# A gated convolution MLP: blocks 0 and 1 scaled in opposite banks, the sums of the first layer split in a new order

## The chip, the cores and the metric

The kernel runs on one core of one Trainium2 chip. The metric is the device time of one execution in microseconds (us). The five engines of the core work side by side, each through its own list of instructions in the order in which it was written: TensorE (PE in the rows; PEld is its loading of weights), VectorE (DVE), ScalarE (ACT), GpSimd (POOL) and SyncE (SP), which here only issues DMAs. They wait for one another through semaphores.

## The reference

Three steps, all in fp32, for 8192 tokens of 192 values. A softmax over 7 taps, for each of 8 heads, weights a causal convolution. Two feed-forward layers follow:

```python
out = np.einsum('bshk,bskhg->bshg', softmax(weight_gen), x_unf)      # 7 taps, 8 heads
xn  = x / np.sqrt(np.mean(x * x, -1) + 1e-06) * rms_g
y   = (silu(xn @ w_gate) * (xn @ w_val)) @ w_out                     # 192 -> 1536 -> 192
h   = y @ w_in                                                       # 192 -> 2048
out = (h * sigmoid(1.702 * h)) @ w_out2                              # 2048 -> 192
```

## The kernel before

The tokens are cut into 16 blocks of 512. TensorE multiplies fp32 numbers as two parts: a high part, rounded to the format `fp32r`, and a low part, the rest. So each operand exists as a pair: `xh`, `xl` and `yh`, `yl` for the first 128 of the 192 values of a token, `xsh`, `xsl` and `ysh`, `ysl` for the other 64, and `h`, `l` for hidden values.

A **unit** `(1, b, m)` is one of 12 pieces of the first layer for block b (function `U1`): TensorE makes `pg` and `pv` in two PSUM banks, ScalarE makes silu of `pg` (line 485), VectorE multiplies by `pv` (`p`, line 489), ScalarE copies the high part (`h`, line 490), VectorE takes the low part (`l`, line 493). A unit `(2, b, i)` is one of 8 pairs of pieces of the second layer (`U2`): two banks `ph`, two silus each (lines 506, 507), one low part each (line 513). The banks of units come from one pool of four, so a unit writes into the banks of the unit two before it, and must wait until that one's have been read. Every product is followed one or two units later by its share of the sums `a` and `b` (`D1`, `D2`).

When the last share of a block's first layer is in, `Y(b)` takes the sums out: ScalarE copies the two halves of bank `b` crosswise into `yt` (lines 537, 538), then bank `a` as `yh` (539), later `yt` as `ysh` (542); VectorE adds bank `b` to `yt` (540) and takes the low parts `yl` (541) and `ysl` (543). `Y(b)` is called at the end of a unit. For blocks from 2 on, two units of the next block's first layer stand between it and the first unit `(2, b, 0)`, which reads its results; the `p` of the first of these two units stands on VectorE behind `Y(b)`, and its banks are those that `(2, b, 0)` writes.

The order of all instructions is that of the code. The list `units` fixes the units; `some` puts steps of other work between their parts on VectorE and ScalarE: decoding the weights (`piece_steps`, lines 95 to 122, while blocks 0 and 1 run) and the convolution of later blocks (`xr`, `acc`, lines 229 and 262). The entries of `splits` run at the end of the unit whose number is their key.

Blocks 0 and 1 open the kernel. Their convolution sums lie in PSUM, tokens 0 and 1 of a row in bank `ac`, tokens 2 and 3 in bank `bc`. `sc(j)` scales them by `ri`: VectorE writes 192 values (line 284), ScalarE another copy of the last 64 (line 287). Then TensorE transposes them into `ax` and `bx`, which use the same two banks (line 351).

Of the kernel before, what the change touches and what calls it, by code (L numbers as in the profile page):

```python
# [9 lines left out]
F32 = mybir.dt.float32  # L10
# [4 lines left out]
ALU = mybir.AluOpType  # L15
# [3 lines left out]
P = 128  # L19
# [5 lines left out]
D = 192  # L25
# [17 lines left out]
def gated_conv_mlp(ctx: ExitStack, tc: tile.TileContext, xp, wg, w1, wo1, w2, wo2, g, out):  # L43
    nc = tc.nc
# [173 lines left out]
    def conv_ops(b):  # L218

        T = BLOCKS[b]  # L220
        Q = T * HEADS
        x = xch[b]
        wn = wn_of[b]
        xr = att.tile([P, T, 2 * P], F32, tag="xr", name=f"xr{b}")
        prod = xr.rearrange("p t c -> p (t c)")[:, 0:Q * GRP]
        ops = []

        def mul(eng, k, dst, j0=0, j1=T):
            eng.tensor_tensor(  # L229
                out=dst.rearrange("p (q g) -> p q g", g=GRP),  # L230
                in0=x[:, (k + j0) * D:(k + j1) * D].rearrange("p (q g) -> p q g", g=GRP),
                in1=wn[:, j0 * HEADS:j1 * HEADS, k:k + 1].to_broadcast([P, (j1 - j0) * HEADS, GRP]), op=ALU.mult)
        cost = 1.04 * Q * GRP + 70
        if b < 2:
            S = T // 2
            sums_of = [pacc.tile([P, NM], F32, tag=f"{n}{b}", name=f"{n}c_{b}") for n in "ab"]
            acc_of = [sums_of[j // S][:, (j % S) * D:(j % S + 1) * D] for j in range(T)]
        else:
            acc = att.tile([P, T, D], F32, tag="acc", name=f"acc{b}")
            acc_of = [acc[:, j] for j in range(T)]  # L240
        if b == 1:
            def tap(k):
                for i, ps in enumerate(sums_of):
                    tag = (("yh", "yl"), ("ysh", "ysl"), ("yh0", "yl0"))[k % 3][i]
                    pr = ytp.tile([P, NM], F32R, tag=tag, name=f"pr{k}_{i}").bitcast(F32)[:, :S * D]
                    mul(nc.gpsimd, k, pr, i * S, (i + 1) * S)
                    nc.tensor.matmul(ps[:, :S * D], ident, pr, start=k == 0, stop=k == TAPS - 1)
            ops += [(cost, lambda k=k: tap(k)) for k in range(TAPS)]
        elif b == 0:
            n = S * D  # L250

            def tap(k):
                for i, ps in enumerate(sums_of):
                    mul(nc.vector, k, prod[:, i * n:(i + 1) * n] if k else ps[:, :n], i * S, (i + 1) * S)
                for i, ps in enumerate(sums_of if k else ()):
                    nc.vector.tensor_tensor(out=ps[:, :n], in0=ps[:, :n], in1=prod[:, i * n:(i + 1) * n], op=ALU.add)
            ops += [(cost, lambda k=k: tap(k)) for k in range(TAPS)]
        else:
            total = acc.rearrange("p t d -> p (t d)")

            def add():
                nc.vector.tensor_tensor(out=total, in0=total, in1=prod, op=ALU.add)  # L262
            for k in range(TAPS):
                ops.append((cost, lambda k=k: mul(nc.vector, k, prod if k else total)))
                if k:
                    ops.append((cost, add))
        ss = sml.tile([P, T], F32, tag="ss", name=f"ss{b}")
        ri = sml.tile([P, T], F32, tag="ri", name=f"ri{b}")

        def sq():  # L270
            room = xr if b != 1 else ytp.tile([P, NM], F32R, tag="yh", name="sq1").bitcast(F32).unsqueeze(1)
            for j in range(T):
                nc.scalar.activation(out=room[:, j if b != 1 else 0, 0:D], in_=acc_of[j], func=AF.Square,
                                     accum_out=ss[:, j:j + 1])
        ops.append((1500, sq))

        def root():
            nc.gpsimd.tensor_scalar(out=ss, in0=ss, scalar1=1.0 / D, scalar2=1e-6,
                                    op0=ALU.mult, op1=ALU.add)
            nc.gpsimd.tensor_tensor(out=ri, in0=ss, in1=half[:, :T], op=ALU.pow)  # L280
        ops.append((500, root))

        def sc(j):
            nc.vector.tensor_scalar_mul(out=xr[:, j, 0:D], in0=acc_of[j], scalar1=ri[:, j:j + 1])
            if b >= TURN:
                return
            nc.scalar.mul(out=xr[:, j, D:2 * P], in_=acc_of[j][:, P:D], mul=ri[:, j:j + 1])
        for j in range(T):
            ops.append((230, lambda j=j: sc(j)))
        xrow[b] = xr  # L290
        return ops
# [79 lines left out]
    yT = {}  # L371
# [144 lines left out]
    def D1(b, m):  # L516
        if m == 0:
            acc1[b] = sums(b, "1_")
        return (acc1[b], O1[m], m, M1, BLOCKS[b] * P, hl1.pop((b, m))), (lambda: Y(b)) if m == M1 - 1 else None
# [6 lines left out]
    def Y(b):  # L526
        N = BLOCKS[b] * P
        pa, pb = acc1.pop(b)
        g = "0" if b in (0, NB - 1) else ""
        W = N if g else NM  # L530
        h = ytp.tile([P, W], F32R, tag="yh" + g, name=f"yh{b}")
        l = ytp.tile([P, W], F32R, tag="yl" + g, name=f"yl{b}")
        sh = ytp.tile([P, W], F32R, tag="ysh" + g, name=f"ysh{b}")
        sl = ytp.tile([P, W], F32R, tag="ysl" + g, name=f"ysl{b}")
        t = zp.tile([P, NM], F32, tag="zb", name=f"yt{b}")

        nc.scalar.copy(t[0:DR, :N], pb[DR:P, :N])
        nc.scalar.copy(t[DR:P, :N], pb[0:DR, :N])
        nc.scalar.copy(h[:, :N], pa[:, :N])
        nc.vector.tensor_tensor(out=t[:, :N], in0=t[:, :N], in1=pb[:, :N], op=ALU.add)  # L540
        nc.vector.tensor_tensor(out=l[:, :N], in0=pa[:, :N], in1=h[:, :N].bitcast(F32), op=ALU.subtract)
        nc.scalar.copy(sh[:, :N], t[:, :N])
        nc.vector.tensor_tensor(out=sl[:, :N], in0=t[:, :N], in1=sh[:, :N].bitcast(F32), op=ALU.subtract)
        yT[b] = (h, l, sh, sl)

    def Z(b, own=None):
        N = BLOCKS[b] * P
# [44 lines left out]
        xt_at[b] = pos[1, b - 1, M1 - 8 if b >= TURN else M1 - 2]  # L592
    xt_by_pos = {v: k for k, v in xt_at.items()}
    splits = {}
    group_of = {b0: gi for gi, (b0, b1) in enumerate(GROUPS)}


# [14 lines left out]
    line = deque()  # L612
# [48 lines left out]
    def some(amounts):  # L661
        for k, a in enumerate(amounts):
            credit[k] += a
        while True:
            ready = [k for k in (0, 1) if streams[k] and credit[k] > 0]
            if not ready:
                return
            for k in ready:
                q = streams[k]
                spent = 0.0  # L670
                while q and credit[k] > 0 and spent < 1500:
                    _, c, f = q.popleft()
                    f()
                    credit[k] -= c
                    spent += c
# [3 lines left out]
    with ExitStack() as order:  # L679
# [49 lines left out]
        soft = {}  # L729
        for i, u in enumerate(units):  # L730
            kind, b, m = u
            if (kind, b, m) == (1, 2, 0):
                early.close()
                late = ctx.enter_context(tc.tile_pool(name="late", bufs=6))
                parts.append((late, late))
                squares.append(ctx.enter_context(tc.tile_pool(name="squares", bufs=1)))
# [40 lines left out]
            while pend and pend[0][0] <= i:  # L777
                _, D_, key = pend.popleft()
                d, f = D_(*key)
# [4 lines left out]
            if i == 0:  # L784
                split = transpose_x(1)
                split(dves=False)
                second()
                split(acts=False)
                third()
                some(todo)  # L790
                some(todo)
            elif i < pos[1, 1, 2]:
                second()
                some(todo)
                third()
                some(todo)
            else:
                some(todo)
                second()
                some(todo)  # L800
                third()
# [4 lines left out]
            else:  # L806

                last = len(units) - 1
# [53 lines left out]
```

## Time and profile before

| | |
|---|---|
| three runs | 1240.44, 1241.30, 1241.46 us; median 1241.3 us |
| the profiled execution | 1240.54 us, of which 1238.6 us are the span from the first to the last instruction |
| busy in the span | PE 1215.7 us (98%), DVE 773.1 us (62%), ACT 650.2 us (52%), POOL 32.3 us (3%) |
| mean granted clock of TensorE | 0.998 of 2.4 GHz |

Busy time is summed over the whole span. It says little of single stages: DVE is busy for 25.6 of the first 31 us and for all 10 us from 30 to 40 us.

### The profile page before, as it was taken

What the parts mean: (1) busy time and instruction counts of PE and PEld (TensorE: products, weight loads), DVE (VectorE), ACT (ScalarE), POOL (GpSimd) and SP (SyncE); (2) the same over time, 40 slices, a digit from 0 to 9 for tenths busy, and PEclk for the clock granted to TensorE, in tenths of its full rate; (3) what the DMA queues carried; (4) which work ended last, traced back from release to release, by engine and by line L of the source; (5) the groups of instructions that cost most, each with busy time, mean ns of one, the idle gap of its engine ahead of it and who ended that gap; (6) DMA issues with size and microseconds to landing.
All of it is one profiled execution on the core that took longest, in us unless ns stands there. A gap on an engine that the chain in (4) does not pass through costs nothing.

```text
span 1238.6 us, 26868 instructions
## 1 busy us (share of the span) xinstructions
PE 1215.7 (98%) x10324; PEld 1100.3 (89%) x10324; DVE 773.1 (62%) x1296; ACT 650.2 (52%) x1279; POOL 32.3 (3%) x53
## 2 busy tenths in 40 slices
PE   5999999999999999999999999999999999999998
PEld 3776999988888999999999989999899998888897
DVE  8989847576657475665747557475664746545432
ACT  4666664555646445454564545446454554544553
POOL 4000000000000000000000000000000000000000
PEclk9999999999999999999999999999999999999999
DMA  5865411001101000110001001001100011000000
GB/s 187 274 182 185 133 57 46 2 1 58 33 16 48 7 25 33 42 34 11 21 33 31 33 16 59 7 26 33 31 33 11 22 33 31 1 15 18 1 14 13
DMA packets 33855, 57.51 MB, mean 46 GB/s; under 512 B 7744, under 2 KB 19392, under 8 KB 33728
## 3 DMA queue, kind: packets, MB, share of 16 engines
q1 hardware_dynamic: 33728, 55.80, 14.5%
q8 instruction: 81, 1.33, 0.4%
q14 instruction: 46, 0.38, 0.1%
HBM read 43.71 MB, written 6.29 MB: 40 GB/s over the span
## 4 chain that ended last, share of the span: by engine, by line
PE 90%; DVE 7%; ACT 2%; issue 1%; DMA 0%; POOL 0%; DVEq 0%; POOLq 0%; ACTq 0%
PE a L380 24%; PE ph L380 21%; PE b L380 16%; PE pv L380 14%; PE pg L380 14%; DVE p L489 1%; DVE l L493 1%; DVE xr L229 1%; DVE dec_a L107 1%; ACT h L490 0%; DVE w L117 0%; DVE dec_s L99 0%; DVE dec_s L111 0%; DVE o L117 0%; DVE acc L262 0%
## 5 line engine op out<-in xcount | busy, mean ns | idle before, releaser
L380 PE MATMUL a<-h,o 64*128 64x512 f32 x1788 | 517.0, 391 | 0.0
L380 PEld LDWEIGHTS a<-h,o 64*128 64x128 f32 x1788 | 326.7, 184 | 14.2
L513 DVE TENSOR_TENSOR l<-p,h 128x512 fp32r<-128x512 f32 x256 | 176.1, 691 | 235.2 <-ACT p L507 233.6
L380 PE MATMUL b<-l,o 64*128 64x512 f32 x896 | 311.2, 393 | 0.1
L380 PE MATMUL a<-l,o 64*128 64x512 f32 x894 | 310.0, 392 | 1.0 <-DVE l L513 0.8
L380 PE MATMUL b<-h,o 64*128 64x512 f32 x896 | 310.4, 392 | 0.0
L506 ACT ACTIVATE h<-ph 128x512 fp32r<-128x512 f32 x256 | 153.9, 601 | 208.5 <-PE ph L380 199.9
L380 PE MATMUL pv<-xh,w 64*128 64x512 f32 x768 | 241.9, 394 | 1.6 <-DVE p L489 1.1
L380 PE MATMUL pg<-xh,w 64*128 64x512 f32 x768 | 242.0, 393 | 1.2 <-ACT w L122 1.2
L380 PE MATMUL ph<-yh,w 64*128 64x512 f32 x1024 | 234.4, 392 | 1.6 <-DVE p L489 1.4
L490 ACT CAST h<-p 128x512 fp32r<-128x512 f32 x192 | 119.4, 622 | 186.3 <-DVE p L489 186.3
L485 ACT ACTIVATE p<-pg 128x512 f32<-128x512 f32 x192 | 114.6, 597 | 164.3 <-PE pg L380 163.7
L489 DVE TENSOR_TENSOR p<-p,pv 128x512 f32<-128x512 f32 x192 | 131.6, 685 | 104.1 <-PE a L380 72.3
L493 DVE TENSOR_TENSOR l<-p,h 128x512 fp32r<-128x512 f32 x192 | 132.6, 691 | 82.9 <-ACT h L490 82.6
L380 PEld LDWEIGHTS a<-l,o 64*128 64x128 f32 x894 | 165.1, 185 | 14.3 <-DVE l L513 2.5
L380 PEld LDWEIGHTS b<-l,o 64*128 64x128 f32 x896 | 165.5, 185 | 8.7 <-DVE l L493 0.5
L380 PEld LDWEIGHTS b<-h,o 64*128 64x128 f32 x896 | 163.9, 185 | 7.7 <-POOLq L395 0.5
L380 PEld LDWEIGHTS ph<-yh,w 64*128 64x128 f32 x1024 | 145.3, 185 | 15.1 <-DVE p L489 2.1
L507 ACT ACTIVATE p<-ph 128x512 f32<-128x512 f32 x256 | 153.9, 601 | 0.0
L380 PEld LDWEIGHTS pv<-xh,w 64*128 64x128 f32 x768 | 140.8, 185 | 14.3 <-DVE p L489 3.8
L380 PE MATMUL ph<-yl,w 64*128 64x512 f32 x512 | 151.2, 391 | 0.0
L380 PE MATMUL pv<-xl,w 64*128 64x512 f32 x384 | 150.5, 392 | 0.0
(117 smaller groups left out, 2098.2 us busy)
## 6 DMA issues: line engine op xcount, KB each, us to landing
x<-in_xp SPq DMA_DIRECT2D x15, 960.0 KB, 4.8
st<-in_w SPq DMA_DIRECT2D x20, 384.0 KB, 4.0
zt<-in_w SPq DMA_DIRECT2D x20, 384.0 KB, 3.4
st<-in_wo SPq DMA_DIRECT2D x14, 384.0 KB, 3.9
zt<-in_wo SPq DMA_DIRECT2D x14, 384.0 KB, 3.4
out_z<-za SPq DMA_DIRECT2D x16, 256.0 KB, 2.2
xl<-raw SPq DMA_DIRECT2D x176, 16.0 KB, 1.8
xsl<-raw SPq DMA_DIRECT2D x176, 16.0 KB, 1.8
```

The lines of the kernel that those rows point to most:

```text
L107: nc.vector.scalar_tensor_tensor(out=ai, in0=ai, scalar=3, in1=t["s"], op0=ALU.logical_shift_left, op1=ALU.bitwise_or)
L229: eng.tensor_tensor(out=dst.rearrange("p (q g) -> p q g", g=GRP), in0=x[:, (k + j0) * D:(k + j1) * D].rearrange("p (q g) -> p q g", g=GRP) ...
L380: ins = nc.tensor.matmul(ps[:, :N], w[rows], x[rows, :N], start=start, stop=stop)
L485: nc.scalar.activation(out=p[:, :N], in_=pg[:, :N], func=AF.Silu)
L489: nc.vector.tensor_tensor(out=p[:, :N], in0=p[:, :N], in1=pv[:, :N], op=ALU.mult)
L490: nc.scalar.copy(h[:, :N], p[:, :N])
L493: nc.vector.tensor_tensor(out=l[:, :N], in0=p[:, :N], in1=h[:, :N].bitcast(F32), op=ALU.subtract)
L506: nc.scalar.activation(out=h[:, :N], in_=ps[j][:, :N], func=AF.Silu, scale=SIG)
L507: nc.scalar.activation(out=p[:, :N], in_=ps[j][:, :N], func=AF.Silu, scale=SIG)
L513: nc.vector.tensor_tensor(out=l[:, :N], in0=p[:, :N], in1=h[:, :N].bitcast(F32), op=ALU.subtract)
```

## The change

Three edits. First, in `sc(j)` of blocks 0 and 1, ScalarE takes token `(j + 2) % 4` while VectorE takes token j, so that the two read different banks. Second, `Y(b)` is written in two parts, `first` (`yh`, `yl`) and `last` (`ysh`, `ysl`). For blocks 0 and 1 both parts are put into `splits` and run at the end of the next unit, only the two crosswise copies and the addition staying where they were. For the other blocks both parts stay in place, `first` ahead of the addition and `last` behind it. Third, at the end of unit 0 the last step of the third weight piece (the copy of its high part, line 122) is run at once, and no longer a unit later.

```diff
@@ sc(j) @@
-            nc.scalar.mul(out=xr[:, j, D:2 * P], in_=acc_of[j][:, P:D], mul=ri[:, j:j + 1])
+            i = (j + T // 2) % T if b < 2 else j
+            nc.scalar.mul(out=xr[:, i, D:2 * P], in_=acc_of[i][:, P:D], mul=ri[:, i:i + 1])
@@ Y(b) @@
         nc.scalar.copy(t[0:DR, :N], pb[DR:P, :N])
         nc.scalar.copy(t[DR:P, :N], pb[0:DR, :N])
-        nc.scalar.copy(h[:, :N], pa[:, :N])
+        yT[b] = (h, l, sh, sl)
+
+        def first():
+            nc.scalar.copy(h[:, :N], pa[:, :N])
+            nc.vector.tensor_tensor(out=l[:, :N], in0=pa[:, :N], in1=h[:, :N].bitcast(F32), op=ALU.subtract)
+
+        def last():
+            nc.scalar.copy(sh[:, :N], t[:, :N])
+            nc.vector.tensor_tensor(out=sl[:, :N], in0=t[:, :N], in1=sh[:, :N].bitcast(F32), op=ALU.subtract)
+        if b > 1:
+            first()
         nc.vector.tensor_tensor(out=t[:, :N], in0=t[:, :N], in1=pb[:, :N], op=ALU.add)
-        nc.vector.tensor_tensor(out=l[:, :N], in0=pa[:, :N], in1=h[:, :N].bitcast(F32), op=ALU.subtract)
-        nc.scalar.copy(sh[:, :N], t[:, :N])
-        nc.vector.tensor_tensor(out=sl[:, :N], in0=t[:, :N], in1=sh[:, :N].bitcast(F32), op=ALU.subtract)
-        yT[b] = (h, l, sh, sl)
+        if b > 1:
+            last()
+        else:
+            splits[at_unit[0] + 1] = lambda: (first(), last())
...
@@ the loop over units @@
+            at_unit[0] = i
...
                 third()
                 some(todo)
                 some(todo)
+                for f in line[0].pop(0):
+                    f()
```

On ScalarE at the start, the list changes in two places: `ac` and `bc` are the banks of the sums of blocks 0 and 1, `w_2` is the third piece's high part, `p_0_1` and `h_0_1` belong to unit (1, 0, 1). Before:

```order
L122 CAST w_0_120<-dec_a 128x384
L287 ACTIVATE xr_156<-ac_157,ri_160 128x64 x2
L287 ACTIVATE xr_156<-bc_158,ri_160 128x64 x2
...
L95 ACTIVATE dec_a<-st 128x384
L485 ACTIVATE p_0_1_413<-pg_1_391 128x512
L490 CAST h_0_1_414<-p_0_1_413 128x512
L122 CAST w_2_259<-dec_a 128x384
```

With the change:

```order
L122 CAST w_0_120<-dec_a 128x384
L288 ACTIVATE xr_156<-bc_158,ri_160 128x64 x2
L288 ACTIVATE xr_156<-ac_157,ri_160 128x64 x2
...
L95 ACTIVATE dec_a<-st 128x384
L122 CAST w_2_259<-dec_a 128x384
L486 ACTIVATE p_0_1_414<-pg_1_392 128x512
L491 CAST h_0_1_415<-p_0_1_414 128x512
```

The two banks have changed places, and the copy of `w_2` stands ahead of the silu and the copy of a unit. VectorE's list is unchanged there.

On VectorE at the end of unit (1, 1, 9), where block 0's sums are taken out. Before:

```order
L493 TENSOR_TENSOR l_1_9_1552<-p_1_9_1550,h_1_9_1551 128x512
L540 TENSOR_TENSOR yt_1576<-yt_1576,b_0_435 128x512
L541 TENSOR_TENSOR yl_1573<-a_0_434,yh_1572 128x512
L543 TENSOR_TENSOR ysl_1575<-yt_1576,ysh_1574 128x512
L229 TENSOR_TENSOR xr_885<-x_663,wraw_311 128x768
L489 TENSOR_TENSOR p_1_10_1620<-p_1_10_1620,pv_10_1585 128x512
L493 TENSOR_TENSOR l_1_10_1622<-p_1_10_1620,h_1_10_1621 128x512
```

With the change:

```order
L494 TENSOR_TENSOR l_1_9_1552<-p_1_9_1550,h_1_9_1551 128x512
L551 TENSOR_TENSOR yt_1576<-yt_1576,b_0_435 128x512
L229 TENSOR_TENSOR xr_885<-x_663,wraw_311 128x768
L490 TENSOR_TENSOR p_1_10_1616<-p_1_10_1616,pv_10_1581 128x512
L494 TENSOR_TENSOR l_1_10_1618<-p_1_10_1616,h_1_10_1617 128x512
L544 TENSOR_TENSOR yl_1573<-a_0_434,yh_1572 128x512
L548 TENSOR_TENSOR ysl_1575<-yt_1576,ysh_1574 128x512
```

`yl` and `ysl` have moved behind the whole next unit, and on ScalarE `yh` and `ysh` likewise behind that unit's `h`. Block 1's move in the same way, behind the two `l` of unit (2, 0, 2).

On VectorE at the end of unit (1, 5, 1), where block 4's sums are taken out. Before:

```order
L493 TENSOR_TENSOR l_5_1_5634<-p_5_1_5632,h_5_1_5633 128x512
L540 TENSOR_TENSOR yt_5644<-yt_5644,b_4_4578 128x512
L541 TENSOR_TENSOR yl_5641<-a_4_4577,yh_5640 128x512
L543 TENSOR_TENSOR ysl_5643<-yt_5644,ysh_5642 128x512
L229 TENSOR_TENSOR xr_5176<-x_5135,wraw_2688 128x768
L489 TENSOR_TENSOR p_5_2_5688<-p_5_2_5688,pv_2_5655 128x512
```

With the change:

```order
L494 TENSOR_TENSOR l_5_1_5634<-p_5_1_5632,h_5_1_5633 128x512
L544 TENSOR_TENSOR yl_5641<-a_4_4577,yh_5640 128x512
L551 TENSOR_TENSOR yt_5644<-yt_5644,b_4_4578 128x512
L548 TENSOR_TENSOR ysl_5643<-yt_5644,ysh_5642 128x512
L229 TENSOR_TENSOR xr_5176<-x_5135,wraw_2688 128x768
L490 TENSOR_TENSOR p_5_2_5688<-p_5_2_5688,pv_2_5655 128x512
```

The low part `yl` and the addition to `yt` have changed places. The same holds for all blocks from 2 to 15; ScalarE's list there is unchanged (`yt`, `yt`, `yh`, `ysh`, and then the silu of the next unit). TensorE's, GpSimd's and SyncE's lists are the same throughout.

## Rows read from the trace of the kernel before

**Rows 1.** The page: span, TensorE's busy time, and the second layer's costliest group.

```profile
span 1238.6 us, 26868 instructions
...
PE 1215.7 (98%) x10324; PEld 1100.3 (89%) x10324; DVE 773.1 (62%) x1296; ACT 650.2 (52%) x1279; POOL 32.3 (3%) x53
...
L380 PE MATMUL ph<-yh,w 64*128 64x512 f32 x1024 | 234.4, 392 | 1.6 <-DVE p L489 1.4
```

**Rows 2.** TensorE's waits from 130 us to the end: total, count, longest.

```profile
PE a L380 <- DVE l L513: 0.5, 1, 0.5
```

**Rows 3.** Windows: length, busy time of PE, PEld, DVE, ACT, POOL, granted clock, DMA.

```profile
24.50:28.50 4.00, 3.98 (x17) 2.59 (x17) 3.35 (x7) 2.36 (x5) 0.00 (x0) 0.57 0.49 133
30.00:40.00 10.00, 8.67 (x72) 7.12 (x72) 10.00 (x25) 6.39 (x15) 0.00 (x0) 1.00 0.68 201
```

**Rows 4.** Timeline of VectorE, scalings of blocks 0 and 1: start, length, [wait before].

```profile
22.88 0.42 DVE L284 TENSOR_SCALAR xr<-ac,ri 128x192 f32<-128x192 f32 x1 [0.38 <-ACT xr L287]
...
24.01 0.42 DVE L284 TENSOR_SCALAR xr<-bc,ri 128x192 f32<-128x192 f32 x1 [0.38 <-ACT xr L287]
...
28.20 0.42 DVE L284 TENSOR_SCALAR xr<-ac,ri 128x192 f32<-128x192 f32 x1 [0.44 <-ACT xr L287]
...
29.32 0.42 DVE L284 TENSOR_SCALAR xr<-bc,ri 128x192 f32<-128x192 f32 x1 [0.38 <-ACT xr L287]
```

**Rows 5.** Timeline of ScalarE and TensorE around the third piece.

```profile
37.44 0.51 ACT L122 CAST w<-dec_a 128x384 fp32r<-128x384 f32 x1
...
38.00 0.50 PE L380 MATMUL pg<-xh,w 64*128 64x512 f32 x1 [1.22 <-ACT w L122]
```

**Rows 6.** Timeline of VectorE and TensorE, block 0's sums.

```profile
108.28 0.69 DVE L540 TENSOR_TENSOR yt<-yt,b 128x512 f32<-128x512 f32 x1 [0.52 <-ACT yt L538]
...
110.27 0.95 DVE L229 TENSOR_TENSOR xr<-x,wraw 128x768 f32<-128x768 f32 x1
111.13 0.68 DVE L489 TENSOR_TENSOR p<-p,pv 128x512 f32<-128x512 f32 x1
...
111.87 0.50 PE L380 MATMUL ph<-yh,w 64*128 64x512 f32 x2 [1.21 <-DVE p L489]
```

**Rows 7.** Timeline of VectorE and TensorE after block 1's sums.

```profile
129.24 1.29 DVE L513 TENSOR_TENSOR l<-p,h 128x512 fp32r<-128x512 f32 x2
...
129.98 0.50 PE L380 MATMUL a<-l,o 64*128 64x512 f32 x1 [0.51 <-DVE l L513]
...
130.59 0.50 PE L380 MATMUL a<-l,o 64*128 64x512 f32 x1
```

**Rows 8.** Timelines of ScalarE, VectorE and TensorE, block 4's sums.

```profile
385.98 0.59 ACT L539 CAST yh<-a 128x512 fp32r<-128x512 f32 x1
386.71 0.62 ACT L542 CAST ysh<-yt 128x512 fp32r<-128x512 f32 x1
...
385.98 0.69 DVE L540 TENSOR_TENSOR yt<-yt,b 128x512 f32<-128x512 f32 x1 [0.51 <-ACT yt L538]
...
387.36 0.69 DVE L543 TENSOR_TENSOR ysl<-yt,ysh 128x512 fp32r<-128x512 f32 x1
387.97 0.95 DVE L229 TENSOR_TENSOR xr<-x,wraw 128x768 f32<-128x768 f32 x1
388.84 0.68 DVE L489 TENSOR_TENSOR p<-p,pv 128x512 f32<-128x512 f32 x1
...
389.70 0.63 PE L380 MATMUL ph<-yh,w 64*128 64x512 f32 x4
```

**Rows 9.** The same two engines, block 13: its `p`, and the product that follows.

```profile
1058.71 0.68 DVE L489 TENSOR_TENSOR p<-p,pv 128x512 f32<-128x512 f32 x1
...
1059.57 0.41 PE L380 MATMUL ph<-yh,w 64*128 64x512 f32 x2
```

**Rows 10.** The same two rows of block 2.

```profile
238.56 0.68 DVE L489 TENSOR_TENSOR p<-p,pv 128x512 f32<-128x512 f32 x1
...
240.28 0.43 PE L380 MATMUL ph<-yh,w 64*128 64x512 f32 x2
```

More of the change, by code (lines that the diff above doesn't have):

```diff
@@ L594, in gated_conv_mlp @@
     splits = {}
+    at_unit = [0]
     group_of = {b0: gi for gi, (b0, b1) in enumerate(GROUPS)}
```

## The prediction

> **What bounds the kernel now.** I read the page first. TensorE is busy for 1215.7 of the 1238.6 us of the span [rows 1], so a change can win at most the 22.9 us that are left, and can lose whatever it adds to TensorE's idle time. Next came TensorE's own waits, to see where those 22.9 us lie: from 130 us to the end there is one, of 0.5 us [rows 2]. So the kernel has two stages. Up to about 131 us TensorE, VectorE and ScalarE wait for one another; afterwards TensorE runs without a gap for 1107 us. Everything that the change could win lies in the first stage. In the second it can only be harmless or harmful, and which of the two depends on how early the other engines deliver. The timelines of the edited places tell that, and they are the rest of the argument.
>
> **The scaling in opposite banks.** VectorE and ScalarE both read the sums, and today they read the same bank by turns: VectorE waits for ScalarE twice in block 0 (0.38 and 0.38 us) and twice in block 1 (0.44 and 0.38 us) [rows 4]. ScalarE's list now begins with the other bank, so these four waits have no cause left: 1.58 us of VectorE's time. This counts, because VectorE is busy without a break right behind them (10.00 of the 10 us from 30 to 40 us [rows 3]); what it starts earlier there it finishes earlier. I take 1.4 us and not 1.58, since ScalarE's next step, a decoding step for which VectorE waits, still stands behind ScalarE's own four scalings. Bounds: 0.8 us, if only block 1's pair of waits (0.82 us) carries through, and 1.6 us.
>
> These waits come from synchronization of the two engines by bank. The Trainium skill (PSUM — Partial Sum Buffer, section on PSUM bank collisions) says that two engines must not be in one bank and the same partitions at once, reads against reads included, while different banks are free. By that rule alone all four waits go, and the sum would be lower by 0.18 us; no row of the kernel before shows the two engines started together in opposite banks.
>
> **The third piece's high part.** TensorE waits 1.22 us at 38.00 us for a copy that ScalarE makes from 37.44 us on, behind a unit's silu and `h` [rows 5]. The copy now stands ahead of them. The banks that this unit needs come free with VectorE's products, which run 1.4 us earlier by the first edit, so TensorE gains its 1.22 us and the slower restart (the first matmul takes 0.50 us [rows 5] against the group's mean of 0.39 [rows 1]: 0.1 us). But this gain and VectorE's 1.4 us are the same time seen on two engines that feed each other, since VectorE has no idle time in this stretch [rows 3]. For both edits together: 1.4 us.
>
> **Block 0's sums in two units.** Today `yl` and `ysl` fill the 1.3 us from the end of `yt` (108.97 us) to `xr` (110.27 us), so `p` ends at 111.81 us and TensorE, which wants its bank, waits 1.21 us [rows 6]. With the change `p` ends at 110.5 us. But what TensorE starts there reads `yh`, `yl`, `ysh` and `ysl`, and these now come behind that unit's `h`: `h` (a copy like `ysh`, 0.62 us [rows 8]) until 111.1 us, `yh` (0.59 us) until 111.7, `yl` and `ysl` on VectorE (0.69 us each, overlapping) until 113.0. The wait for the bank becomes a wait for the data, which ends at 111.7 us; VectorE's list as a whole is some 0.2 us ahead. I take 0.2 us, with bounds of -0.3 and +1.2 us.
>
> **Block 1's sums in two units.** Here two units lie between the sums and their reader as well, but the wait falls elsewhere: the low parts of the second layer, at 129.24 us, stand behind `yl` and `ysl`, and TensorE waits for the first (0.51 us) and then for the second, 0.61 us after it [rows 7] where pairs of matmuls follow each other at 0.24 us (0.63 less 0.39 us [rows 1, 8]). Moved ahead of `yl` and `ysl` they come 1.3 us earlier, and TensorE gains 0.51 + 0.37 + 0.1 us = 1.0 us. About 0.3 us return, since the next unit's low parts come only 0.2 us earlier than now. So 0.7 us, from 0 to 1.0.
>
> The first stage gains 1.4 + 0.2 + 0.7 = 2.3 us.
>
> **The other fourteen blocks.** In these nothing is split; only `yl` and the addition to `yt` change places on VectorE. `yl` needs `yh`, ScalarE's third copy, and the addition only the second. Today the addition runs beside `yh` (both start at 385.98 us), and `ysh` follows at 386.71 and `ysl` at 387.36 us [rows 8]. With the change VectorE waits for `yh` until 386.57 us; `yl` starts at 386.60; the addition, at the 0.61 us that lie between VectorE's neighbours here (`ysl` to `xr` [rows 8]), at 387.21 and ends at 387.90; `ysh` takes 0.62 us until 388.55; `ysl` starts at 388.58. That is 1.22 us later, and everything behind it on VectorE moves with it: `xr` and `p`, which ends at 390.74 instead of 389.52 us. ScalarE is held as well, since the silu of the next unit stands behind `ysh`; it would end at about 389.1, so VectorE stays the later one.
>
> `p` is waited for: TensorE's next unit starts at 389.70 us [rows 8] and writes the bank that `p` reads. It is the same kind of wait as the one of 1.21 us in block 0, where the row names `p` as its releaser [rows 6]. Today `p` is 0.18 us early, so no wait shows. With the change TensorE waits until 390.79: 1.08 us, and 0.1 us for the restart, 1.18 us.
>
> Nine blocks (4 to 7, 9 to 13) have a step of the convolution between `ysl` and `p`, as block 4; the last has `p` ending at 1059.39 and TensorE at 1059.57 us [rows 9], 0.18 us of margin again. Four blocks (2, 3, 8, 14) have none; block 2's `p` ends at 239.24 and TensorE comes at 240.28 us [rows 10], a margin of 1.04 us, so the wait is about 0.2 us and 0.1 for the restart. Block 15's sums fall among units of the second layer, where no `p` follows; I take nothing for it.
>
> TensorE does not win this back, since it has no other idle time in this stage [rows 2]: 9 x 1.18 + 4 x 0.3 = 11.8 us. Bounds of the delay: 0.6 us, the wait for `yh` alone, if the steps behind it closed up (0.5 us each for the nine, nothing for the four: 4.6 us in all); and 1.4 us, if each block's second `p` is late as well (1.4 and 0.5 us: 14.6 us).
>
> **The sum.** The profiled execution took 1240.5 us. 1240.5 - 2.3 + 11.8 = 1250.0 us. It lies 0.8 us below the median of the three runs; halfway between the two references the forecast is 1250.4 us.
>
> **The rivals.**
>
> *The delay is absorbed (faster).* If TensorE had slack in front of each second-layer unit, only the first stage would count: 1240.5 - 2.3 = 1238.2 us, somewhat over or under 0.2% below the median, and 1237 with the upper bounds. For it speaks that no wait for `p` shows after 130 us [rows 2]. Against it stand the two margins of 0.18 us [rows 8, 9]. It decides at that number: a delay of `p` under 0.18 us is free, and each 0.1 us above it costs 0.9 us over nine blocks.
>
> *The delay is half as long.* If `ysh` and `ysl` follow more closely, `p` comes 0.6 to 0.8 us late: 4.6 to 6.5 us are added, 1243 to 1245 us. What speaks against it is that `ysh` reads the sum in `yt`, so it can't start before the addition's end, and the chain of three steps is then the one that I added up.
>
> *TensorE's clock falls in each new wait.* After a long idle time at the start, the granted clock was 0.57 over the 4.0 us from 24.5 to 28.5 us [rows 3], mostly the level of 1.2 GHz, where TensorE did 57% of the work it could have done: 1.7 us lost. Nine times that would be 15.5 us: 1265 us. Against it stands the stretch from 30 to 40 us, which holds the wait of 1.22 us and has a clock of 1.00 [rows 3, 5]. The Trainium skill (TensorE: Matmul & The Clock Gate, Part 1) says that the throttled state is the default and that activity releases it; by that rule every new wait is a risk, and the row says that one of this length is not.
>
> **How the numbers follow.** A run of this kernel can be told from no change at about 0.2%, 2.5 us. Chances: 0.80 for the forecast, 0.09 for the absorbed delay (two thirds of it faster, the rest the same), 0.07 for the half delay (0.02 of it the same), 0.04 for the fallen clock. That gives faster 0.06, same 0.05, slower 0.89. The range for 8 in 10 goes halfway to the bounds on the low side: 8.2 us of loss (between 4.6 and 11.8) and 3.1 us of gain (between 2.3 and the 3.8 us of the upper bounds together) give 1240.5 - 3.1 + 8.2 = 1245.6 us. On the high side it takes both bounds, 0.5 us of gain and 14.6 us of loss: 1254.6 us. It leaves out the absorbed delay, most of the half delay and the fallen clock, together less than 2 in 10.
>
> **What the profile of the changed kernel would show.** If I am right, VectorE's four waits of rows 4 are gone and the wait at 38 us too; around 110 us TensorE waits for `yh` and not for `p`; and from 230 us on TensorE shows a wait of about 1.1 us, released by `p`, in front of the first second-layer unit of nine blocks, with the addition to `yt` some 0.6 us behind `yl`. What would make it wrong: a `p` that is still in time there, because VectorE or ScalarE catches up between `ysl` and `p`, or waits of TensorE in these nine places that are shorter than 0.5 us.

## The result, and the profile after

| | before | after |
|---|---|---|
| median of 4 runs each | 1241.38 us | 1251.72 us |
| lowest and highest | 1240.44, 1242.57 us | 1250.65, 1252.47 us |
| profiled execution, its span | 1240.54 us, 1238.6 us | 1250.65 us, 1248.9 us |

The changed kernel is slower: ratio 1.0082, 95% interval 1.0065 to 1.0100, against 1250.4 us forecast, with a range of 1245.6 to 1254.6 us.

The page after: span, TensorE's busy time, and the second layer's group of [rows 1], whose idle time has grown from 1.6 to 8.8 us.

```profile
span 1248.9 us, 26883 instructions
...
PE 1220.9 (98%) x10324; PEld 1150.2 (92%) x10324; DVE 772.4 (62%) x1296; ACT 651.4 (52%) x1279; POOL 32.2 (3%) x53
...
L381 PE MATMUL ph<-yh,w 64*128 64x512 f32 x1024 | 245.9, 396 | 8.8 <-DVE p L490 7.2
```

All waits of TensorE after, over the whole span (total, count, longest); line numbers of the body are one higher than before.

```profile
PE ac L247 <- POOL pr L229: 8.1, 1, 8.1
PE ph L381 <- DVE p L490: 7.2, 9, 0.9
PE ax L352 <- ACT xr L288: 3.7, 1, 3.7
PE ph L381 <- ACT yh L543: 1.6, 1, 1.6
PE pv L381 <- DVE p L490: 1.1, 5, 0.3
PE pg L381 <- ACT xh L362: 0.3, 1, 0.3
```

Nine waits for `p` stand where the second stage had none [rows 2], the wait for `w` at 38 us [rows 5] is gone, and one for `yh` has taken the place of block 0's wait for `p` [rows 6].

The timeline of VectorE after: the scalings of blocks 0 and 1, the `p` of unit (1, 0, 1), and block 4's sums.

```profile
22.03 0.74 DVE L284 TENSOR_SCALAR xr<-ac,ri 128x192 f32<-128x192 f32 x2 [0.38 <-POOL ri L280]
22.73 0.74 DVE L284 TENSOR_SCALAR xr<-bc,ri 128x192 f32<-128x192 f32 x2
...
26.16 0.73 DVE L284 TENSOR_SCALAR xr<-ac,ri 128x192 f32<-128x192 f32 x2
26.81 0.73 DVE L284 TENSOR_SCALAR xr<-bc,ri 128x192 f32<-128x192 f32 x2
...
29.74 0.68 DVE L490 TENSOR_TENSOR p<-p,pv 128x512 f32<-128x512 f32 x1
...
384.60 0.69 DVE L544 TENSOR_TENSOR yl<-a,yh 128x512 fp32r<-128x512 f32 x1 [1.12 <-ACT yh L543]
385.21 0.68 DVE L551 TENSOR_TENSOR yt<-yt,b 128x512 f32<-128x512 f32 x1
386.63 0.69 DVE L548 TENSOR_TENSOR ysl<-yt,ysh 128x512 fp32r<-128x512 f32 x1 [0.74 <-ACT ysh L547]
387.24 0.95 DVE L229 TENSOR_TENSOR xr<-x,wraw 128x768 f32<-128x768 f32 x1
388.11 0.68 DVE L490 TENSOR_TENSOR p<-p,pv 128x512 f32<-128x512 f32 x1
```

ScalarE's scalings of block 0 after:

```profile
22.17 0.52 ACT L288 ACTIVATE xr<-bc,ri 128x64 f32<-128x64 f32 x2
22.81 0.52 ACT L288 ACTIVATE xr<-ac,ri 128x64 f32<-128x64 f32 x2
```

None of the four waits of [rows 4] is left: each pair of scalings is one group of two without a gap, and in block 0 ScalarE reads one bank while VectorE reads the other. The Trainium skill (PSUM — Partial Sum Buffer, section on PSUM bank collisions) says that different banks are free of each other; the rows agree. In block 4 `yl` waits 1.12 us for `yh`, the addition follows 0.61 us behind it, `ysl` waits for `ysh`, and `p` follows `xr` at once: the order that the prediction wrote out for [rows 8].

The timeline of TensorE after, around the third piece, block 0 and block 4.

```profile
35.65 0.39 PE L381 MATMUL a<-l,o 64*128 64x512 f32 x1
35.80 0.39 PE L381 MATMUL pg<-xh,w 64*128 64x512 f32 x1
...
109.39 0.73 PE L381 MATMUL ph<-yh,w 64*128 64x512 f32 x4 [1.60 <-ACT yh L543]
...
112.10 0.62 PE L381 MATMUL a<-h,o 64*128 64x512 f32 x1
...
113.93 0.39 PE L381 MATMUL a<-h,o 64*128 64x512 f32 x1
...
387.75 0.39 PE L381 MATMUL ph<-yh,w 64*128 64x512 f32 x1
388.84 0.73 PE L381 MATMUL ph<-yh,w 64*128 64x512 f32 x3 [0.70 <-DVE p L490]
```

The unit that stood at 38.00 us starts at 35.80 us without a wait. In block 4 the first product goes through at 387.75 us, because the other of the two banks is free already; the next one, into the bank that `p` reads, comes when `p` ends (388.11 + 0.68 us). So the wait is listed as 0.7 us, though the products fall 1.1 us behind.

At 112.10 us a single product takes 0.62 us instead of 0.39. Windows after (length, busy time of PE, PEld, DVE, ACT, POOL, granted clock, DMA share, GB/s) tell why:

```profile
24.00:28.00 4.00, 3.54 (x19) 2.07 (x17) 3.97 (x11) 3.05 (x8) 0.00 (x0) 0.60 0.71 232
...
111.00:113.00 2.00, 2.00 (x14) 1.53 (x12) 2.00 (x6) 0.24 (x1) 0.00 (x0) 0.50 0.00 0
...
380.00:700.00 320.00, 316.80 (x2707) 303.15 (x2706) 196.13 (x305) 165.66 (x312) 4.80 (x8) 1.00 0.09 26
```

Behind block 0's wait the clock is at 0.50, the level of 1.2 GHz. In the 320 us that hold four of the nine waits it is 1.00.

**Where the time went.** Both traces hold the same 10324 matmuls in the same order (but for pairs that start together, whose two can change places), so each can be set against its twin: start after minus start before, and of these differences the median over a stretch (minus: earlier than before).

| stretch of the trace before, us | after | scaling alone | piece alone | both, no split | with block 1's split | with both splits, old order |
|---|---|---|---|---|---|---|
| 95 to 105 | -2.22 | -1.36 | -0.02 | -2.20 | -1.58 | -1.54 |
| 114 to 118 | -0.84 | -0.27 | 1.06 | -1.11 | -0.50 | -1.67 |
| 119 to 123 | -2.24 | -1.37 | -0.02 | -2.20 | -1.59 | -1.73 |
| 136 to 150 | -3.03 | -1.35 | 0.00 | -2.22 | -2.38 | -2.54 |

(The other columns are experiments, below.) The changed kernel is 3.0 us ahead when the first stage is over. Then it loses 1.11 to 1.18 us at each of the nine blocks (10.2 us in all), 0.24 to 0.34 us at blocks 2, 3, 8 and 14 (1.1 us), 0.06 us at block 15, and 1.9 us in small amounts between the blocks. It ends 10.2 us behind.

### The profile page after: what moved, and what is told of

Same layout as the page of the kernel before. It is cut to its first block, busy times and chain, and to the rows that moved or that the text cites. A ratio compares the mean times of both kernels' runs of the same rounds, so it can differ in the third digit from the quotient of the medians.

```text
span 1248.9 us, 26883 instructions
## 1 busy us (share of the span) xinstructions
PE 1220.9 (98%) x10324; PEld 1150.2 (92%) x10324; DVE 772.4 (62%) x1296; ACT 651.4 (52%) x1279; POOL 32.2 (3%) x53
## 4 chain that ended last, share of the span: by engine, by line
PE 89%; DVE 9%; ACT 1%; issue 1%; DMA 0%; POOL 0%; DVEq 0%; POOLq 0%
PE a L381 24%; PE ph L381 21%; PE b L381 15%; PE pg L381 15%; PE pv L381 13%; DVE p L490 2%; DVE xr L229 1%; DVE l L494 1%; DVE dec_a L107 1%; DVE acc L262 1%; DVE w L117 0%; DVE dec_s L111 0%; DVE dec_s L99 0%; ACT h L491 0%; DVE o L117 0%
## 5 line engine op out<-in xcount | busy, mean ns | idle before, releaser
L381 PE MATMUL ph<-yh,w 64*128 64x512 f32 x1024 | 245.9, 396 | 8.8 <-DVE p L490 7.2
L381 PEld LDWEIGHTS ph<-yh,w 64*128 64x128 f32 x1024 | 148.0, 185 | 25.2 <-DVE p L490 12.2
L381 PE MATMUL ph<-yl,w 64*128 64x512 f32 x512 | 158.7, 393 | 0.1
L381 PE MATMUL pg<-xl,w 64*128 64x512 f32 x384 | 150.6, 392 | 0.0
```

Of the source, the lines that this page charges most:

```text
L381: ins = nc.tensor.matmul(ps[:, :N], w[rows], x[rows, :N], start=start, stop=stop)
```

## The experiments

The theory: the swap of `yl` and the addition makes `p` late in blocks 2 to 15 and costs some 13 us, while the first stage gains 2 to 3 us, nearly all from the scaling and from block 1's sums. The rivals: that the waits for `p` come from the shift of the first stage and not from the swap; that TensorE's clock falls in them; that each of the other edits has a gain of its own. Medians are of 11 runs unless said otherwise, each beside the kernel before on the same chip (1240.7 to 1240.9 us).

### The old order back in blocks 2 to 15

```diff
-        if b > 1:
-            first()
+        if not (b < 2):
+            nc.scalar.copy(h[:, :N], pa[:, :N])
         nc.vector.tensor_tensor(out=t[:, :N], in0=t[:, :N], in1=pb[:, :N], op=ALU.add)
-        if b > 1:
+        if not (b < 2):
+            nc.vector.tensor_tensor(out=l[:, :N], in0=pa[:, :N], in1=h[:, :N].bitcast(F32), op=ALU.subtract)
             last()
```

> All of the change except that blocks 2 to 15 keep the old order (the addition to yt ahead of yl). Theory (the swap of yl and the addition in these blocks delays p by 1.2 us and costs 13.2 us in all, as the two traces' offsets between 131 us and 1145 us show; everything before 131 us gains 3.1 us): 1241.4 - 3.1 = 1238.3 us, and TensorE shows no wait for p after 130 us. Rival (the waits for p come from the first stage's shift, which lets the blocks' convolution steps and transfers meet differently): the nine waits stay, about 1251 us. By the prediction's own first-stage sum of 2.3 us it would be 1239.1 us.

1238.38 us, ratio 0.9981 (0.9972 to 0.9990). From 130 us to the end TensorE's list of waits is empty. The loss is the swap's.

### The swap alone

```diff
         nc.scalar.copy(h[:, :N], pa[:, :N])
-        nc.vector.tensor_tensor(out=t[:, :N], in0=t[:, :N], in1=pb[:, :N], op=ALU.add)
-        nc.vector.tensor_tensor(out=l[:, :N], in0=pa[:, :N], in1=h[:, :N].bitcast(F32), op=ALU.subtract)
+        nc.vector.tensor_tensor(out=l[:, :N], in0=pa[:, :N], in1=h[:, :N].bitcast(F32), op=ALU.subtract)
+        nc.vector.tensor_tensor(out=t[:, :N], in0=t[:, :N], in1=pb[:, :N], op=ALU.add)
```

(in blocks 2 to 15 only)

> The kernel before with only the swap of yl and the addition to yt in blocks 2 to 15. Theory: 1241.4 + 13.2 = 1254.6 us, with nine waits of TensorE for p of 0.8 to 0.9 us each and a granted clock of 1.00 in the windows that hold them. Rival (the waits come from the first stage's shift): 1241.4 us. Second rival (the clock falls in these waits): half-speed pairs of matmuls (0.42 us instead of 0.23 us) behind them, and over 1257 us.

1253.46 us (4 runs), ratio 1.0105 (1.0091 to 1.0119). TensorE's waits from 130 us on, and windows around block 4's wait:

```profile
PE ph L380 <- DVE p L489: 7.7, 9, 0.9
PE a L380 <- DVE l L513: 0.5, 1, 0.5
```

```profile
390.00:392.00 2.00, 1.08 (x10) 0.57 (x7) 1.95 (x3) 0.27 (x2) 0.00 (x0) 1.00 0.01 4
392.00:396.00 4.00, 4.00 (x34) 3.31 (x36) 2.68 (x4) 2.27 (x5) 0.00 (x0) 1.00 0.00 0
```

TensorE is idle for nearly half of the first window, and the clock stays at 1.00 in it and behind it. The swap costs 12.7 us by the medians, and with the 2.4 us that the other edits gain this is the change's whole effect (12.7 - 2.4 = 10.3 us, as measured).

### The swap with an earlier `yh`

The swap as above, and ScalarE's copy `yh` moved ahead of its two copies into `yt`, in blocks 2 to 15:

```diff
+        nc.scalar.copy(h[:, :N], pa[:, :N])
         nc.scalar.copy(t[0:DR, :N], pb[DR:P, :N])
         nc.scalar.copy(t[DR:P, :N], pb[0:DR, :N])
-        nc.scalar.copy(h[:, :N], pa[:, :N])
```

> The kernel before with yl ahead of the addition in blocks 2 to 15 as in the change, and besides ScalarE's copy yh ahead of its two copies to yt, so that VectorE doesn't wait for yh behind them. Theory (each block pays what p's delay exceeds 0.18 us, and a restart of 0.1 us): the addition waits for the second yt copy as before and ends behind yl, ysl starts 0.6 us later than before instead of 1.25, TensorE waits 0.4 us in nine blocks and not in four: 1240.8 + 9 x 0.5 = 1245.3 us. Rival (the order of the two on VectorE costs as such, however early yh is): 1253.5 us. Second rival (a delay of 0.6 us is still hidden): 1240.8 us.

1244.75 us (6 runs), ratio 1.0033 (1.0020 to 1.0045). VectorE's and TensorE's timelines in block 4:

```profile
385.40 0.68 DVE L542 TENSOR_TENSOR yl<-a,yh 128x512 fp32r<-128x512 f32 x1
386.48 0.69 DVE L543 TENSOR_TENSOR yt<-yt,b 128x512 f32<-128x512 f32 x1 [0.40 <-ACT yt L540]
387.85 0.69 DVE L549 TENSOR_TENSOR ysl<-yt,ysh 128x512 fp32r<-128x512 f32 x1 [0.69 <-ACT ysh L548]
...
389.33 0.68 DVE L489 TENSOR_TENSOR p<-p,pv 128x512 f32<-128x512 f32 x1
```

```profile
389.74 1.05 PE L380 MATMUL ph<-yh,w 64*128 64x512 f32 x4
```

`ysl` is 0.49 us later than in [rows 8], and `p` ends at 390.01 us, 0.27 us past the start of the group that needs its bank. The group of four then takes 1.05 us, where [rows 8] have 0.63. The second stage's list of waits shows none of this: the loss of 0.31 to 0.44 us at each of the nine blocks stands inside the group. In blocks 2, 3, 8 and 14, where `p` has room, TensorE loses 0.00 to 0.05 us. So the price follows the delay of `p` beyond its margin, not the order as such.

### The scaling alone, the third piece alone, both

The first is the change's edit in `sc(j)` on the kernel before, the second the two lines at the end of unit 0, the third both; `Y` is as before in all three.

> The kernel before with only ScalarE's scaling in the opposite banks. Theory (each of VectorE's four waits costs 0.46 to 0.5 us and not the 0.38 us that is listed, and VectorE sets the pace until 131 us): VectorE's p of unit (1,0,1) starts at 29.8 instead of 31.9 us, TensorE still waits for the third piece's high part for about 1.2 us near 36 us, and the end comes 2.2 us earlier: 1239.2 us. Rival (TensorE's wait for the third piece is the bound, and the edit only lengthens it): TensorE is 1.0 us ahead behind that wait, 1240.4 us.

> The kernel before with only the early copy of the third piece's high part. Theory (the same time as the banks' edit, seen on another engine; VectorE without idle time sets the pace): TensorE's wait of 1.22 us at 38.00 us goes or is taken over by a wait for VectorE, TensorE's lead over the kernel before is under 0.3 us by 60 us, end 1241.4 us. Rival (a gain of its own): TensorE stays 1.2 us ahead to the end, 1240.2 us.

> The kernel before with the opposite banks and the early third piece, and Y as it was for all blocks. Theory (the two edits give the same time, the early copy nothing beyond the banks' edit): 1239.1 us as with the banks alone; no wait for w at 36 us, but the wait for p near 110 us (1.2 us) and the waits for l near 127 us are there. Rival (the copy adds its 1.2 us once VectorE is ahead): 1238 us.

1239.13 us (ratio 0.9986, 0.9977 to 0.9995), 1240.66 us (0.9999, 0.9991 to 1.0008) and 1238.54 us (0.9983, 0.9974 to 0.9992). With the early copy alone TensorE passes the place of the wait at 36.56 us and meets the next one soon behind it:

```profile
36.56 0.40 PE L380 MATMUL pg<-xh,w 64*128 64x512 f32 x1
...
39.29 0.49 PE L380 MATMUL b<-l,o 64*128 64x512 f32 x1 [0.44 <-DVE l L493]
```

Its lead is 1.44 us there, 0.41 us at 60 us (under 0.3 was expected) and 0.02 us at 95 us (the table). With the scaling alone the wait for `w` is gone too, against my expectation, because the copy itself comes at 36.08 instead of 37.44 us [rows 5]; the unit starts at 36.64 us. So the two edits do not add up, as predicted. The third kernel's median is 0.6 us lower than the first's; the intervals (1.1 us either way) do not tell whether the early copy gives that, or the clock, to which the last two experiments come.

### One split at a time

Both other edits and the old order in blocks 2 to 15, with only block 1's sums split, and then only block 0's: `b < 2` in the code above becomes `b == 1`, and then `b == 0`.

> As the kernel with the old order in blocks 2 to 15 (1238.4 us), but only block 1's sums split in two units, block 0's left in place. Theory (the gain of the splits, some 0.7 us, is block 1's; block 0's only turns a wait for p into one for yh): 1238.4 us, with a wait of 1.2 us for p near 110 us and none for l near 127 us. Rival (block 0's split gives the gain, since it puts VectorE ahead): 1239.1 us.

> The same with only block 0's sums split. Theory: 1239.0 us, with a wait of 1.6 us for yh near 109 us and the waits for l near 127 us (0.5 us and one behind it) as before. Rival (the gain is block 0's): 1238.4 us.

1238.28 us (ratio 0.9978, 0.9970 to 0.9987) and 1239.44 us (0.9988, 0.9979 to 0.9996). Alone the medians tell little at this size, but the table does: between 119 and 136 us the lead grows by 0.79 us with block 1's split, by 0.81 us with both, and by at most 0.02 us with none; with block 0's alone it goes from -1.87 to -1.84 us. Over block 0's place (95 to 119 us) it grows by at most 0.01 us with no split of block 0, and by 0.02 to 0.19 us with it. The gain is block 1's, as the theory had it.

### Keeping TensorE busy at the start

The leads at 95 us differ (1.36 to 2.22 us) between kernels that have the same scaling, and so does VectorE's `p` of unit (1, 0, 1). Both go with TensorE's clock while it makes block 0's eight transposes. These in the changed kernel, and in the version with block 1's split:

```profile
23.38 0.66 PE L352 MATMUL ax<-ident,xr 128*128 128x128 f32 x4 [3.70 <-ACT xr L288]
23.87 0.60 PE L352 MATMUL bx<-ident,xr 128*128 128x128 f32 x4
```

```profile
23.38 1.12 PE L352 MATMUL ax<-ident,xr 128*128 128x128 f32 x4 [3.71 <-ACT xr L288]
24.29 1.06 PE L352 MATMUL bx<-ident,xr 128*128 128x128 f32 x4
```

The granted clock from 23 to 25 us is 0.95 in the first and 0.50 in the second. The transposes are slow in four kernels (scaling alone, both splits with the old order, either split alone): there `p` starts at 30.31 to 30.48 us (with the scaling alone I had expected 29.8), and the lead at 95 us is 1.36 to 1.68 us. They are fast in the changed kernel and with both edits but no split: `p` at 29.74 and 29.80 us, the lead 2.22 and 2.20 us. Among the slow ones the lead is 1.36 us without the early third piece and 1.54 to 1.68 us with it; so of the 0.84 us between the scaling alone and both edits, 0.2 to 0.3 us can be the early copy's, and the rest goes with the clock. The clock of a longer stretch does not sort them: from 24 to 28 us it is 0.66 with block 0's split alone, where `p` is late, and 0.60 in the changed kernel. TensorE is idle ahead of the transposes, from 19.7 to 23.4 us. This edit fills that time, in the version with only block 1's sums split:

```diff
         run(conv[TAPS + 2:])
+        for _ in range(30):
+            nc.tensor.matmul(wn0[:, 0:P], ident, ident, start=True, stop=True)
         split = transpose_x(0)
```

> The version with only block 1's sums split (old order in blocks 2 to 15, both other edits), and 30 matmuls of 128x128 whose result nobody reads put on TensorE between 19.7 us and the first transposes at 23.4 us, where it is idle in all kernels so far. Theory (what the edits on the scaling and the piece give varies between 1.5 and 2.2 us with TensorE's clock from 23 to 29 us, which falls to the level of 1.2 GHz some time after that idle stretch): the clock stays at 1.00 from 23 to 29 us, TensorE's lead over the kernel before is 2.2 us or more at 60 us instead of 1.6, and the median is 0.6 us or more under the 1238.3 us of the same version without them. Rival (the clock there has nothing to do with the idle stretch, or VectorE hides it): clock near 0.5 again, or no gain, 1238.3 us.

1240.50 us, ratio 0.9998 (0.9989 to 1.0007). Each matmul stands in the trace as two, and TensorE reached the transposes only at 26.78 us (timeline):

```profile
20.08 6.86 PE L729 MATMUL wn<-ident 128*128 128x128 f32 x60
26.78 0.60 PE L352 MATMUL ax<-ident,xr 128*128 128x128 f32 x4
```

The clock was 1.00 from 23 to 33 us, but the overrun of 3.4 us hid what that gave. With 13 instead of 30:

> The same with 13 of these matmuls instead of 30: the 30 ran as 60 passes and held TensorE until 26.7 us, 3.3 us past the first transposes' place; 26 passes end near 23.0 us. Theory (the clock falls only behind the idle stretch): granted clock 1.00 from 23 to 29 us, VectorE's p of unit (1,0,1) at 29.7 us or earlier, TensorE 2.2 us or more ahead of the kernel before at 60 us and 3.0 us behind block 1, the median 0.6 us or more under 1238.3 us: 1237.7 us or less. Rival (the clock isn't the cause of the spread in the first stage's gain): 1238.3 us with the clock at 1.00.

1237.66 us (9 runs), ratio 0.9975 (0.9965 to 0.9984). Its windows:

```profile
24.00:28.00 4.00, 3.46 (x24) 1.90 (x22) 3.94 (x10) 3.06 (x8) 0.00 (x0) 1.00 0.68 231
...
111.00:113.00 2.00, 2.00 (x20) 1.45 (x16) 2.00 (x6) 0.63 (x2) 0.00 (x0) 1.00 0.00 0
```

The clock is at 1.00 in both, the transposes take 0.66 and 0.60 us, `p` starts at 29.79 us (29.7 or earlier was expected), and the lead is 2.55 us at 60 us, 2.19 us at 95 us and 2.99 us at 136 us. It is the best version: 3.2 us faster than the kernel before on its chip. The Trainium skill (TensorE: Matmul & The Clock Gate, Part 1) says that the throttled state is the default and that activity releases it; this pair of traces agrees (0.50 from 24 to 28 us without the filler, 1.00 with it). The median is 0.6 us lower than without, just what was expected, but from another chip and with an interval as wide as that; the clock, the length of the transposes and the place of `p` carry this, not the median. Two kernels without the filler had fast transposes as well, so what it gives is the better of two cases each time, as far as two traces show.

## Why the prediction was right, point by point

**The scaling in opposite banks: right in kind, too small.** The four waits went. I took 1.4 us, at most 1.6; VectorE's `p` of unit (1, 0, 1) came 2.2 us earlier (29.74 us after). Before:

```profile
24.82 1.10 PE L351 MATMUL bx<-ident,xr 128*128 128x128 f32 x4
```

```profile
31.94 0.68 DVE L489 TENSOR_TENSOR p<-p,pv 128x512 f32<-128x512 f32 x1
```

Two things were missing. A listed wait is less than it costs: in block 1 the second scalings of the two banks start 1.12 us apart in [rows 4], and the two groups after 0.65 us apart, 0.47 us for a listed 0.38. And I had no term for the clock at the transposes. Before, the second bank's transposes came with the clock at 0.50 (25 to 27 us) and took 1.10 us; after, they came ahead of that fall and took 0.60 us, though from 24.5 to 28.5 us both traces show 0.57 [rows 3]. So `xsl` follows `xl` at 0.66 instead of 0.89 us, and still at 0.85 us in the four kernels that have the new scaling and slow transposes. In these four `p` came 1.5 to 1.6 us earlier than before, close to what I had taken; the other 0.6 to 0.7 us of the changed kernel's trace is luck with the clock.

**The third piece's high part: right.** The wait went, and the edit alone gives 1240.66 against 1240.77 us: the same time, seen on two engines.

**Block 0's sums: right.** The wait for `p` became one for `yh` (1.60 us against 1.21 [rows 6]); the gain is 0 to 0.2 us, 0.2 had been taken. The clock's fall at 111 us, in this and in four of the experiments' traces, costs 1.1 to 1.4 us of the lead by 118 us, and all of it is back by 123 us: VectorE, busy for all 10 us from 111 to 121 us after, sets the pace there.

**Block 1's sums: right.** 0.8 us; 0.7 had been taken.

**Blocks 2 to 15: right.** Per block 1.11 to 1.18 us in the nine (taken: 1.18) and 0.24 to 0.34 us in the four (0.3). The margin of 0.18 us, read at two of the nine, is 0.14 to 0.19 us at all of them in the trace before. `ysl` came 1.27 us later against TensorE than before (1.22). The wait is listed as 0.7 to 0.9 us and not as 1.1, since one product slips ahead into the other bank. Block 15 costs 0.06 us where I took nothing. The 1.9 us between the blocks, some 0.1 us in each, I did not foresee, and no experiment says what they are; the swap alone has them too.

**The sum.** 2.3 us of gain and 11.8 of loss were forecast; the traces have 3.0 and 13.3 us, and the medians of the two halves 2.4 and 12.7 us. Both terms were low, the loss by more (0.7 and 1.5 us by the traces, 0.1 and 0.9 us by the medians), so a part of the error cancelled, and the net loss of 9.5 us that was forecast came out as 10.3 us.

**The rivals.** The absorbed delay falls with the swap alone. The half delay did not come (`ysl` 1.27 us late); where the earlier `yh` produced one, of 0.49 us, 4.0 us were added, where that rival had 4.6 to 6.5. The fallen clock does not follow these waits: the windows that hold the nine, to 1100 us, have 1.00. The clock fell in or behind the idle stretch of 2.9 to 4.1 us at the start, in every trace without the filler, and in some around 111 us, where the length of the wait does not decide it: of two kernels with the same wait for `yh` there (1.60 and 1.58 us) one has 0.50 from 111 to 113 us, the other (the old order back) 1.00.

## What to carry to other kernels

Ask of each instruction on an engine's list by how much its result is early for the engine that sets the end; here a margin of under 0.2 us at nine places decided 10 us, and no list of waits shows a margin. Of two neighbours put first the one whose input is there first: an addition that could run beside a copy was put behind a reader of that copy. When a rewrite for an opening stage also changes the order in the loop behind it, keep the old order there: here the opening gained 2.4 us once, and the new order, which ran fourteen times, cost 12.7 us.

## What the hardware showed that I had not expected

A wait of a few tenths need not be listed: with the earlier `yh`, each of nine blocks lost 0.31 to 0.44 us, and the list of the second stage had no wait for `p`, since the first product of the group, which goes through at once, covers the gap until the next; only the length of the group (in block 4 1.05 instead of 0.63 us) told.

The clock at the start differs from trace to trace of like programs, and 0.7 us of VectorE's time hung on whether it had fallen when eight transposes ran: the clock was 0.95 or 0.50 from 23 to 25 us in the two traces shown, and the transposes took 1.1 or 2.0 us in all. Filler work of 3.06 us in the idle stretch ahead of them brought 1.00, and the clock was at 1.00 around 111 us too in both kernels that had it; whether that is due to the filler or chance, two traces do not tell.
